# Cluster attention and a squared-ReLU MLP on one core: the three low bits of each weight are made on GpSimd, and VectorE joins them in one operation

## The chip, the cores and the metric

The kernel runs on one core of one Trainium2 chip. The metric is the device time in microseconds (us) of one execution; lower is better. Five engines of the core each work through their own queue of instructions in order: PE (TensorE, matrix products), DVE (VectorE), ACT (ScalarE), POOL (GpSimd) and SP (SyncE, which here issues the data transfers). They wait for one another by semaphores.

## The reference

Four batches of eight heads attend over 768 positions with a head size of 64; a query sees only the keys whose nearest of 16 centroids is its own. The result, 3072 rows of 512, goes through a two-layer MLP.

```python
q_assign = argmax(q_n . c_n);  k_assign = argmax(k_n . c_n)      # per head
scores = where(q_assign == k_assign, q @ k.T / sqrt(D), -1e9)
x = (softmax(scores) @ v).transpose(0, 2, 1, 3).reshape(B * S, H * D)
h = x @ w_in                       # w_in: 512 x 2048
g = s * relu(h) ** 2 + b
out = (g @ w_out).astype(float32)  # w_out: 2048 x 512
```

The weights `w_in` and `w_out` arrive as 64-bit floats (two 32-bit words each), all else in 32 bits. [...]

## The kernel before

**Weights.** The two matrices are cut into 16 pairs of tiles (`wi`, `wo`), 32 tiles of 128 x 512 values. `weights()` takes tile after tile through four steps: `fetch` loads both words of every value (512 KB) into a staging buffer; `rebase` (L213) lets ACT read the high words, 8 bytes apart, and put them as rebased floats into the tile; `narrow` (L217) lets DVE shift the tile left by three bits (L219) and then shift the low word right by 29 and OR it in (L220); `bound` (L223) takes absolute values on ACT (L227, L229) and column sums and maxima on PE and DVE (L232, L233). There are four staging buffers: three of the tag `stage`, and for every fourth tile the idle buffer `gs`. So a load has to wait until `narrow` of the tile four places ahead of it has read its buffer. When the last tile is through, scale factors for both matrices are known (`finish_w_in`, `finish_w_out`, into `glob`), and `wsplit` then splits each tile into two 16-bit parts (ACT L277, DVE L279), which the MLP's products use.

**Attention.** Work comes in 192 units (batch, chunk of 256 positions, pair of heads, tile of 128 rows, head). A unit's scores are made on PE (L476), their row maximum on DVE (L486), their exponential on ACT (L496). For the first 16 units the result is turned on PE into the one buffer `turned` (L520), half by half; each half is then copied by ACT (L525) and its remainder taken by DVE (L526). Later units are turned by DMA (L530) after a GpSimd subtraction (L528). `prep_k`, `prep_q` and `prep_v` load and split keys, queries and values and make the one-hot cluster codes (`onehot`, L298 to L304), which are written by GpSimd or DVE and turned by DMA into `KB` and `QB`.

**MLP.** Step m runs beside unit m + 21 (`LAG`): `mlp_in` (PE L632), `mlp_relu` (ACT L639 to L642), `mlp_gl` (POOL L647), `mlp_out` (PE L659). Its first step needs the first 16 units' output and the scale factors of the weights.

**Order.** The loop at the kernel's end names the work in program order. A scheduler then sets every engine's order by priorities and an estimated timeline of its own, so an edit at one place can move instructions of the whole first part of the program. SP's loads and DMA transposes stand in one queue in order.

Of the kernel before, what the change touches and what calls it, by code (L numbers as in the profile page):

```python
# [12 lines left out]
U32 = mybir.dt.uint32  # L13
AF = mybir.ActivationFunctionType
ALU = mybir.AluOpType
# [11 lines left out]
def tile_cluster_attention_mlp(ctx, tc, q, k, v, cent, w_in, w_out, s_in, b_in, out):  # L27
# [12 lines left out]
    V = nc.vector  # L40
    G = nc.gpsimd
# [171 lines left out]
    def rebase(d):  # L213
        hw = d["st"][:, :, :, 1].bitcast(F32)
        A.activation(d["w"], hw, AF.Prelu, scale=2.0 ** -112, alpha=-(2.0 ** 32))

    def narrow(d):  # L217
        c = d["w"].bitcast(I32)
        V.tensor_scalar(c, c, 3, None, op0=ALU.logical_shift_left)  # L219
        V.scalar_tensor_tensor(c.bitcast(U32), d["st"][:, :, :, 0].bitcast(U32), 29, c.bitcast(U32),  # L220
                               op0=ALU.logical_shift_right, op1=ALU.bitwise_or)

    def bound(d):  # L223
        w, p, ft = d["w"], d["p"], d["ft"]
# [14 lines left out]
    def weights():  # L239
        live = {}  # L240
        for i in range(2 * NF + 4):
            if 0 <= i - 4:
                bound(live[i - 4])
                narrowed[0] += 1
            if 0 <= i - 3 < 2 * NF:
                rebase(live[i - 3])
                narrow(live[i - 3])
            if i < 2 * NF:
                live[i] = fetch(i)
            if i < 2 * NF + 3:  # L250
                yield
# [571 lines left out]
```

## Time and profile before

| | |
|---|---|
| median of 3 runs | 946.23 us (946.06 to 949.96) |
| the profiled execution's own time | 952.97 us |
| its span, first to last instruction | 951.3 us |
| mean granted TensorE clock | 0.954 |
| busy share of the span: PE, DVE, ACT, POOL | 87%, 68%, 75%, 58% |

The profiled execution is one run of the program, 6.7 us above the median of the timed runs; 1.7 us of its time lie outside the span. A row of a timeline reads: start in us, duration in us, engine, line, operation, what is written from what, count, and in brackets the idle time of the engine just ahead with what ended it. A row of a group reads: engine and form, count, busy time and mean duration. In the table by stage each engine has its busy time and, in brackets, its number of instructions, followed by the granted clock of PE, the DMA engines' share and GB/s. "SPq" is SP's queue of transfers.

### The profile page before, as it was taken

To read this page: it belongs to the slowest core of one execution; us is meant where nothing else is said; L and a number is where in the kernel's file an instruction comes from. 1 tells how busy PE (TensorE), PEld (TensorE's weight loads), DVE (VectorE), ACT (ScalarE), POOL (GpSimd) and SP (SyncE) were. 2 spreads that over 40 slices of the span, in tenths; PEclk is the share of its full clock that TensorE was granted. 3 is DMA by queue.
4 is the path that set the end of the run, shared out by engine and by line. 5 is a ranking of instruction groups with operands and counts; after the bars stand their busy time and mean duration, and the time that the engine had idled before them with its cause. 6 is when DMAs were issued, how large, how long until landed. Compare 5 with 4: busy or idle time off the path is not lost.

```text
span 951.3 us, 22936 instructions
## 1 busy us (share of the span) xinstructions
PE 830.0 (87%) x8697; PEld 580.1 (61%) x8697; DVE 651.1 (68%) x1684; ACT 715.4 (75%) x1405; POOL 548.0 (58%) x580
## 2 busy tenths in 40 slices
PE   0565667886999889999999989999999899999997
PEld 0353445554676657767666657667766676676764
DVE  7689978798786766758967766667877565654100
ACT  3469866777688678788878868888888788888543
POOL 3010115667577567677677747767776676666321
PEclk9975697999999999999999999999999999999999
DMA  5898513767897897876887978979968777577200
GB/s 165 215 262 283 161 38 80 174 145 150 168 168 146 172 204 123 167 162 139 178 169 164 201 156 148 171 145 197 178 140 182 145 123 159 115 140 140 46 23 23
DMA packets 437759, 144.25 MB, mean 152 GB/s; under 512 B 405392, under 2 KB 434064, under 8 KB 437648
## 3 DMA queue, kind: packets, MB, share of 16 engines
q1 hardware_dynamic: 437648, 142.78, 70.7%
q8 instruction: 68, 1.11, 0.5%
q14 instruction: 43, 0.35, 0.1%
HBM read 35.69 MB, written 6.29 MB: 44 GB/s over the span
## 4 chain that ended last, share of the span: by engine, by line
PE 45%; DVE 23%; DMA 12%; ACT 7%; issue 5%; POOL 2%; SPq 1%; POOLq 0%; DVEq 0%; ACTq 0%
PE h L632 16%; PE acc L659 16%; PE sc L476 6%; DVE ssm L486 5%; DMA qn<-in_q_dram 3%; DMA PT<-ph 2%; PE sc L574 2%; DMA kn<-in_k_dram 2%; DMA vn<-in_v_dram 2%; PE sc L576 2%; PE sc L575 2%; ACT p L496 1%; DVE wis L279 1%; DVE qa L196 1%; DMA wst<-in_moe_w_in_dram 1%
## 5 line engine op out<-in xcount | busy, mean ns | idle before, releaser
L528 POOL TENSOR_TENSOR ph<-p,ph 128x768 f16<-128x768 f32 x176 | 297.0, 1688 | 129.7 <-ACT ph L126 71.1
L632 PE MATMUL h<-x,wis 128*128 128x256 f16 x2304 | 291.9, 276 | 16.1 <-ACT r L639 9.7
L659 PE MATMUL acc<-wos,gs 128*128 128x512 f16 x1152 | 299.7, 381 | 4.1 <-POOL gs L647 2.8
L632 PEld LDWEIGHTS <-wis 128*128 128x128 f16 x2304 | 222.5, 99 | 72.3 <-issue 18.0
L496 ACT ACTIVATE p<-sc,ssm,qsm 128x768 f32<-128x768 f32 x192 | 188.5, 982 | 2.0
L647 POOL TENSOR_TENSOR gs<-r,gs 128x256 f16<-128x256 f32 x192 | 136.5, 712 | 88.1 <-ACT r L642 79.4
L486 DVE TENSOR_REDUCE ssm<-sc 128x1 f32<-128x768 f32 x192 | 181.7, 947 | 2.8 <-PE sc L476 2.6
L659 PEld LDWEIGHTS <-gs 128*128 128x128 f16 x1152 | 101.4, 98 | 79.4 <-POOL gs L647 5.6
L493 ACT ACTIVATE ssm<-ssm,lift,qsm 128x1 f32<-128x1 f32 x192 | 73.1, 381 | 91.3 <-DVE ssm L486 90.1
L126 ACT ACTIVATE ph<-p 128x768 f16<-128x768 f32 x164 | 136.7, 833 | 1.3 <-DMA PT<-ph 0.2
L639 ACT ACTIVATE r<-h,cf 128x256 f32<-128x256 f32 x192 | 89.2, 465 | 57.8 <-PE h L632 54.5
L574 PE MATMUL sc<-vh,PT 128*128 128x65 f16 x1032 | 117.4, 195 | 6.9 <-DMA PT<-ph 6.8
L576 PE MATMUL sc<-vh,PT 128*128 128x65 f16 x1032 | 117.9, 193 | 0.0
L575 PE MATMUL sc<-vl,PT 128*128 128x64 f16 x1032 | 117.5, 192 | 0.0
L476 PE MATMUL sc<-KA,QA 128*128 128x384 f16 x384 | 98.9, 340 | 19.2 <-ACT p L496 13.8
L574 PEld LDWEIGHTS <-PT 128*128 128x128 f16 x1056 | 99.1, 98 | 22.8 <-DMA PT<-ph 10.1
L575 PEld LDWEIGHTS <-PT 128*128 128x128 f16 x1056 | 98.5, 99 | 11.8 <-issue 0.5
L476 PE MATMUL sc<-KB,QB 128*128 128x384 f16 x384 | 99.2, 340 | 6.9 <-DMA QB<-qb 6.9
L576 PEld LDWEIGHTS <-PT 128*128 128x128 f16 x1056 | 98.7, 97 | 1.3
L580 DVE TENSOR_SCALAR ssm<-sc 128x1 f32<-128x1 f32 x172 | 26.1, 152 | 84.5 <-PE sc L576 83.7
L642 ACT ACTIVATE r<-r 128x256 f32<-128x256 f32 x192 | 78.8, 410 | 2.9
L641 ACT ACTIVATE gs<-r 128x256 f16<-128x256 f32 x192 | 78.9, 411 | 2.7
(176 smaller groups left out, 1145.0 us busy)
## 6 DMA issues: line engine op xcount, KB each, us to landing
wst<-in_moe_w_in_dram SPq DMA_DIRECT2D x16, 512.0 KB, 5.1
kn<-in_k_dram SPq DMA_DIRECT2D x16, 384.0 KB, 4.3
qn<-in_q_dram SPq DMA_DIRECT2D x24, 256.0 KB, 3.3
vn<-in_v_dram SPq DMA_DIRECT2D x16, 384.0 KB, 4.3
out_dram<-o SPq DMA_DIRECT2D x12, 512.0 KB, 3.6
wst<-in_moe_w_out_dram SPq DMA_DIRECT2D x8, 512.0 KB, 5.7
gs<-in_moe_w_out_dram SPq DMA_DIRECT2D x8, 512.0 KB, 4.9
PT<-ph SPq DMA_TRANSPOSE x176, 3.4
```

Of the source, the lines that this page charges most:

```text
L126: A.activation(dst, src, AF.Copy)
L476: last_score[0] = nc.tensor.matmul(sc[:, e, :HALF], X[:, col, :], y[:, h * S + e * HALF : h * S + (e + 1) * HALF], start=st, stop=not st)
L486: last_max[0] = V.tensor_reduce(SM[i // 4][:, 0, j : j + 1], U[i]["sc"], axis=AX.XY, op=ALU.max, negate=True)
L496: last_exp[0] = A.activation(p.rearrange("p (a b) -> p a b", a=2), u["sc"], AF.Exp, bias=bi, scale=u["scale"], **total)
L528: G.tensor_tensor(u["ph"][:, 1, :], u["p"], u["ph"][:, 0, :], op=ALU.subtract)
L574: nc.tensor.matmul(o1, PT[:, kt, :], vh[:, h, kt, : D + 1], start=(kt == 0), stop=False)
L575: nc.tensor.matmul(o, PT[:, kt, :], vl[:, h, kt, :], start=False, stop=False)
L576: nc.tensor.matmul(o1, PT[:, T + kt, :], vh[:, h, kt, : D + 1], start=False, stop=(kt == T - 1))
L632: nc.tensor.matmul(ph[:, :CW], WSP[ft][0][:, wl, kt, :], XS[(b, c, kt)][:, :, xl, :], start=(i == 0), stop=(i == len(terms) - 1))
L639: A.activation(r, ph[:, :CW], AF.Relu, scale=MS[(b, c)][0])
L647: G.tensor_tensor(g[:, 1, :], r, g[:, 0, :], op=ALU.subtract)
L659: nc.tensor.matmul(acc[:, t, :], g[:, gl, rows], WSP[ft][1][:, wl, :], start=(ft == 0 and gl + wl == 0), stop=(ft == NF - 1 and gl == 1))
```

## The change

For each of the 32 weight tiles, `rebase` now also lets GpSimd turn the low words into the integers 0 to 7, in place in the staging buffer: a multiply and an add on the low word read as an unsigned integer, written as a 32-bit integer (rounded; the factor keeps the result in range). `narrow` is one DVE operation in place of two: it shifts the tile left by three bits and ORs these integers in.

```diff
@@ rebase, narrow @@
     def rebase(d):
         hw = d["st"][:, :, :, 1].bitcast(F32)
         A.activation(d["w"], hw, AF.Prelu, scale=2.0 ** -112, alpha=-(2.0 ** 32))
+        lw = d["st"][:, :, :, 0]
+        G.tensor_scalar(lw, lw.bitcast(U32), 0.9375 * 2.0 ** -29, -0.03125, op0=ALU.mult, op1=ALU.add)
 
     def narrow(d):
         c = d["w"].bitcast(I32)
-        V.tensor_scalar(c, c, 3, None, op0=ALU.logical_shift_left)
-        V.scalar_tensor_tensor(c.bitcast(U32), d["st"][:, :, :, 0].bitcast(U32), 29, c.bitcast(U32),
-                               op0=ALU.logical_shift_right, op1=ALU.bitwise_or)
+        V.scalar_tensor_tensor(c.bitcast(U32), c.bitcast(U32), 3, d["st"][:, :, :, 0].bitcast(U32),
+                               op0=ALU.logical_shift_left, op1=ALU.bitwise_or)
```

Lines below the added ones move by one (L486 becomes L487, and so on). The scheduler also orders the engines anew. Three places matter.

The first is DVE, where the first four weight tiles (`wi0`, `wo0`, `wi1`, `wo1`) come up, beside the one-hot codes of the first keys and queries (`om`, `oe`, `oo`). Before:

```order
L219 TENSOR_SCALAR wi0_257<-wi0_257 128x512
L302 TENSOR_REDUCE om_k0_0_296<-oe_k0_0_297 128x12
L219 TENSOR_SCALAR wo0_260<-wo0_260 128x512
L220 SCALAR_TENSOR_TENSOR wi0_257<-wst_0_258,wi0_257 128x512
L303 TENSOR_TENSOR oo_k0_0_298<-oe_k0_0_297,om_k0_0_296 128x192
L220 SCALAR_TENSOR_TENSOR wo0_260<-wst_1_261,wo0_260 128x512
L219 TENSOR_SCALAR wi1_263<-wi1_263 128x512
L304 TENSOR_SCALAR kb_132<-oo_k0_0_298 128x12x64
L220 SCALAR_TENSOR_TENSOR wi1_263<-wst_2_264,wi1_263 128x512
L219 TENSOR_SCALAR wo1_269<-wo1_269 128x512
L220 SCALAR_TENSOR_TENSOR wo1_269<-gs_128,wo1_269 128x512
L298 TENSOR_REDUCE om_q0_0_0_323<-pq_0_0_0_306 128x8
```

After, from the end of the second key's codes on:

```order
L305 TENSOR_SCALAR kb_1_140<-oo_k0_1_360 128x12x64
L487 TENSOR_REDUCE ssm_0_389<-sc_0_384 128x1
L221 SCALAR_TENSOR_TENSOR wo0_260<-wo0_260,wst_1_261 128x512
L487 TENSOR_REDUCE ssm_0_389<-sc_1_453 128x1
L221 SCALAR_TENSOR_TENSOR wi1_263<-wi1_263,wst_2_264 128x512
L221 SCALAR_TENSOR_TENSOR wo1_269<-wo1_269,gs_128 128x512
L128 COPY PT_0_462<-turned_135 128x384
```

Three of the four tiles' operations moved from among the first codes to behind the first row maxima (`ssm`).

The second place is DVE at the last weight tile (`wo15`). `sc_13` are the scores of unit 13, `PT_9` is the turned result of unit 9, in two halves. Before:

```order
L526 TENSOR_TENSOR PT_9_1020<-turned_135,PT_9_1020 128x384
L233 TENSOR_REDUCE w1_129<-pw_14_1332 128x1
L219 TENSOR_SCALAR wo15_1306<-wo15_1306 128x512
L486 TENSOR_REDUCE ssm_12_1153<-sc_13_1220 128x1
L220 SCALAR_TENSOR_TENSOR wo15_1306<-gs_128,wo15_1306 128x512
L233 TENSOR_REDUCE w1_129<-pw_15_1414 128x1
L526 TENSOR_TENSOR PT_9_1020<-turned_135,PT_9_1020 128x384
```

After:

```order
L527 TENSOR_TENSOR PT_8_927<-turned_135,PT_8_927 128x384
L221 SCALAR_TENSOR_TENSOR wi15_1298<-wi15_1298,wst_30_1299 128x512
L487 TENSOR_REDUCE ssm_12_1153<-sc_12_1148 128x1
L234 TENSOR_REDUCE w1_129<-pw_13_1289 128x1
L221 SCALAR_TENSOR_TENSOR wo15_1306<-wo15_1306,gs_128 128x512
L527 TENSOR_TENSOR PT_8_927<-turned_135,PT_8_927 128x384
```

The last weight tile now stands ahead of the second half of unit 8 and of unit 13's maximum, where it stood ahead of the second half of unit 9 and behind that maximum.

The third place is POOL in the middle of the weight stage. Before, the one-hot codes of keys 2 and 3 (`oe_k0_2`, `kb_2`, `oe_k0_3`, `kb_3`) stand there one behind the other:

```order
L301 TENSOR_TENSOR oe_k0_2_442<-oe_k0_2_442,rev_73 128x192
L304 TENSOR_SCALAR kb_2_143<-oo_k0_2_443 128x12x64
L301 TENSOR_TENSOR oe_k0_3_518<-oe_k0_3_518,rev_73 128x192
L304 TENSOR_SCALAR kb_3_146<-oo_k0_3_519 128x12x64
```

After:

```order
L302 TENSOR_TENSOR oe_k0_2_442<-oe_k0_2_442,rev_73 128x192
L217 TENSOR_SCALAR wst_6_483<-wst_6_483 128x512
L217 TENSOR_SCALAR gs_128<-gs_128 128x512
L305 TENSOR_SCALAR kb_2_143<-oo_k0_2_443 128x12x64
L217 TENSOR_SCALAR wst_8_559<-wst_8_559 128x512
L217 TENSOR_SCALAR wst_9_567<-wst_9_567 128x512
L217 TENSOR_SCALAR wst_10_629<-wst_10_629 128x512
L217 TENSOR_SCALAR gs_128<-gs_128 128x512
L302 TENSOR_TENSOR oe_k0_3_518<-oe_k0_3_518,rev_73 128x192
L217 TENSOR_SCALAR wst_12_671<-wst_12_671 128x512
L305 TENSOR_SCALAR kb_3_146<-oo_k0_3_519 128x12x64
```

The new operations stand between the code operations, which wait for DVE; each code operation that waits holds up the weight tiles behind it.

## The prediction

> **What bounds the kernel now.** I read first the table by stage, then the chain of waits of the weight stage, then SP's own waits, then single rows. The stages are the first codes (26 to 41 us), the weights (41 to 114), the way to the first MLP step (114 to 146), the splitting of the weights beside the MLP (146 to 240), and the rest.
>
> ```profile
> core 0: us, PE busy (x) PEld busy (x) DVE busy (x) ACT busy (x) POOL busy (x), PEclk, DMA share, GB/s
> 26.00:41.00 15.00, 5.29 (x55) 3.20 (x56) 11.32 (x29) 6.53 (x14) 0.00 (x0) 1.00 0.75 186
> 41.00:114.00 73.00, 45.46 (x361) 33.67 (x360) 64.50 (x149) 57.82 (x119) 7.07 (x9) 0.68 0.86 251
> 114.00:146.00 32.00, 20.83 (x234) 15.35 (x232) 25.25 (x70) 20.58 (x38) 5.56 (x6) 0.82 0.14 34
> 146.00:240.00 94.00, 75.48 (x764) 50.30 (x762) 81.94 (x183) 66.49 (x128) 61.30 (x53) 0.90 0.65 141
> 240.00:945.00 705.00, 679.26 (x7258) 475.74 (x7256) 447.35 (x1189) 553.88 (x1091) 463.97 (x470) 0.99 0.74 147
> ```
>
> From 240 us on PE is busy 96% of the time (679.26 of 705) and sets the end, whatever the change does. It can pay only by bringing that stage forward. Between 41 and 114 us, where all but four of the 32 tiles are narrowed, DVE is the fullest engine (64.50 of 73.00, 88%), but ACT has 79% and the DMA engines 86%, while POOL has 10%. The chain of waits of this stage says how these share the path:
>
> ```profile
> 42.08 4.57 DMA wst<-in_moe_w_in_dram
> ...
> 63.34 6.73 DMA wst<-in_moe_w_out_dram
> ...
> 92.33 5.29 DMA wst<-in_moe_w_out_dram
> ```
>
> Five times it runs through a load (the first, the longest and the last are shown), 25.5 us of the 73 in all; in the other 47 us it is on DVE, ACT and PE. The loads in turn wait for DVE to give back a staging buffer:
>
> ```profile
> SPq L86 <- DVE wi L220: 21.6, 10, 6.1
> SPq L86 <- DVE wo L220: 13.9, 7, 4.4
> ```
>
> So the weight stage is a ring: load, ACT, DVE, buffer free, load. A shorter DVE part shortens the ring, but the loads in it stay.
>
> **What is removed.** The 32 shifts (L219) go; the join (L220, now L221) stays with as many elements and inputs, so I give it the same price.
>
> ```profile
> L219 DVE TENSOR_SCALAR wi<-wi x16: 408/416/826, 27.0 to 109.1; 128x512 int32<-128x512 int32 x16
> L220 DVE SCALAR_TENSOR_TENSOR wi<-wst,wi x16: 671/679/843, 27.9 to 110.8; 128x512 uint32<-128x512 uint32 x16
> 63.19 0.41 DVE L219 TENSOR_SCALAR wi<-wi 128x512 int32<-128x512 int32 x1
> 63.53 0.34 DVE L303 TENSOR_TENSOR oo_k<-oe_k,om_k 128x192 f16<-128x192 f32 x1
> ```
>
> A shift is 0.41 us long, but the next instruction starts 0.34 us after it (63.19 to 63.53), so 0.34 is what each takes from DVE: 10.9 us for 32 (16 of `wi`, as many of `wo`).
>
> Four of them lie at 27 to 31 us. There the next thing DVE has to do waits for others:
>
> ```profile
> 37.76 1.82 DVE L486 TENSOR_REDUCE ssm<-sc 128x1 f32<-128x768 f32 x2 [1.76 <-PE sc L476]
> 41.43 0.56 DVE L128 COPY PT<-turned 128x384 f32<-128x384 f32 x1 [1.85 <-PE turned L520]
> ```
>
> DVE is idle for 1.76 and 1.85 us right behind, so these four are worth nothing, and the three joins that the change puts behind the first maxima fit into the 1.85. Without that cover the four shifts would be worth 1.4 us.
>
> Of the other 28 (9.5 us), nine start while the chain is on one of the five loads, from the first to the last of these:
>
> ```profile
> 59.93 0.41 DVE L219 TENSOR_SCALAR wi<-wi 128x512 int32<-128x512 int32 x1
> ...
> 95.88 0.42 DVE L219 TENSOR_SCALAR wi<-wi 128x512 int32<-128x512 int32 x1
> ```
>
> They only lengthen a queue that is not the last to end. Nineteen lie on the chain's other pieces: 19 x 0.34 = **6.5 us gained**. The bounds are 0 (the loads alone set the pace) and 10.9 (all 32 count).
>
> **What is added.** 32 operations on GpSimd, 128x512, one input, 32-bit integers 8 bytes apart. The trace has no such operation; the nearest rows are the last three of these, and the first is ACT's for the same tile:
>
> ```profile
> L215 ACT ACTIVATE wi<-wst 128x512 f32<-128x512 f32 x16 | 10.6, 666 | 7.4 <-DMA wst<-in_moe_w_in_dram 7.3
> L304 POOL TENSOR_SCALAR qb<-oo_q 128x512 f16<-128x512 f16 x23 | 14.2, 618 | 16.2 <-DVE oo_q L303 9.1 <-DVE ssm L580 2.9 <-DVE vm L443 2.1
> L128 POOL CAST ph<-p 128x768 f16<-128x768 f32 x3 | 2.5, 823 | 10.5 <-ACT p L496 10.5
> L528 POOL TENSOR_TENSOR ph<-p,ph 128x768 f16<-128x768 f32 x176 | 297.0, 1688 | 129.7 <-ACT ph L126 71.1 <-issue 18.1 <-PE acc L659 16.8
> ```
>
> The multiply-add on as many 16-bit elements takes 618 ns, and a cast that reads 32 bits is no slower per element (823 for 768). With two inputs it is 1688 for 768, 1125 ns for 512. I take 0.65 us, near the one-input rows, with 0.62 and 1.13 as ends. ACT needs 0.67 us for the tile, at the same time, so at this price the join waits no longer than it waited for ACT. The cover is gone if GpSimd is late: its queue is nearly empty (7.07 us of 73), but the operations behind a code operation that waits for DVE wait too, and behind a late join stand maxima and remainders that ACT and PE wait for.
>
> GpSimd at work costs DVE something. Here both meet:
>
> ```profile
> 105.61 0.67 POOL L599 TENSOR_TENSOR xn<-xs,xn 128x256 f16<-128x256 f32 x1 [25.90 <-ACT xn L596]
> 106.23 1.08 POOL L394 COPY qa<-qb 128x512 f16<-128x512 f16 x1
> ...
> 105.63 1.20 DVE L220 SCALAR_TENSOR_TENSOR wo<-gs,wo 128x512 uint32<-128x512 uint32 x1
> 106.76 0.83 DVE L219 TENSOR_SCALAR wi<-wi 128x512 int32<-128x512 int32 x1
> ```
>
> The join, 0.68 alone, takes 1.20 when it starts with a GpSimd operation of 0.67; the next GpSimd copy takes 1.08, and the shift behind it 0.83 in place of 0.41. [...] With the new work POOL is busy 7.07 + 28 x 0.65 = 25.3 us of some 68, 37%. A join then meets it in 37% of cases and waits half an operation, 0.33: 0.12 us each, on the chain 19 x 0.12 = **2.3 us lost**; the removed shifts no longer collide, but they met GpSimd seldom.
>
> [...]
>
> **What is moved.** At the last weight tile DVE has done one maximum and two remainders fewer than before (unit 13's maximum, halves of units 8 and 9). The weights no longer wait for these; they now come afterwards, where the turning of one half after another sets the pace:
>
> ```profile
> 49.28 0.87 DVE ssm L486
> 114.17 0.47 DVE PT L526
> ...
> 113.30 0.67 DVE L220 SCALAR_TENSOR_TENSOR wo<-gs,wo 128x512 uint32<-128x512 uint32 x1
> ...
> 121.17 0.56 DVE L526 TENSOR_TENSOR PT<-turned,PT 128x384 f16<-128x384 f32 x1 [0.92 <-ACT PT L525]
> 122.89 0.56 DVE L526 TENSOR_TENSOR PT<-turned,PT 128x384 f16<-128x384 f32 x1 [1.16 <-ACT PT L525]
> ```
>
> On the chain they take 0.87 and 2 x 0.47 us, 1.8 in all, by which the last join (113.30) comes earlier. Behind it a half takes 1.72 us, with DVE idle for 0.92 and 1.16. Two more cost 3.5 us: net **1.7 us lost** (0 if DVE's gaps take them up, 3.5 if the weights don't end earlier by the 1.8).
>
> **The sum.** 6.5 - 2.3 - 1.7 = 2.5 us. Against the profiled execution that is 951.3 to 948.8 of span, 952.97 to 950.5 of its time. The timed runs stand 6.7 us below this execution; the same 2.5 us off their median of 946.23 give **943.7 us**. About 0.5% (4.7 us) is what a measurement can tell here from no change, so this counts as none. I leave what the scheduler's other reorderings between 146 and 240 us do at zero, with some 3 us either way: DVE's 82 of 94 us there are the same operations, in slightly other places.
>
> **Rivals.**
>
> *DVE is the only bound.* The 88%, and SP's 35.5 us of waiting for DVE, speak for it; the five loads on the chain speak against. Then all 28 shifts pass on, the collisions cost 2.3, and the halves are made up for in DVE's gaps: 9.5 - 2.3 = 7.2, **939.0 us**.
>
> *GpSimd is dear.* If its operation takes 1.13 us, the two-input price, POOL is busy 38.7 us of 73 (53%). Each of the 28 joins waits 0.53 x 0.57 = 0.30 us, 8.5 us on all, and at the five places where the chain goes from a load to ACT the tile is ready 0.46 us later than by ACT, 2.3. With the moved halves: 6.5 - 8.5 - 2.3 - 1.7 = -6.0, 6 us slower, **952.2 us**. It decides from about 0.85 us an operation on, where 19 x 0.19 + 5 x 0.18 + 1.7 eats the 6.5. For it speaks that no 32-bit integer row on POOL stands in the trace; against it the two one-input rows, which agree. [...]
>
> *Loads and ACT set the pace.* DMA at 86% and ACT at 79% leave little: if the stage keeps its 73 us, the moved halves alone count, with half their price **947.1 us**. The loads that waited 35.5 us for DVE speak against.
>
> That the change does not do what it says I leave out: the order shows 32 new operations on POOL and none of the shifts.
>
> **The numbers.** My forecast has 0.38 (its own range 941 to 946.5), DVE as only bound 0.32, GpSimd dear 0.18, loads and ACT 0.12. Faster by over 0.5% (below 941.5): nearly all of the second and a little of the first, 0.34. Slower by over 0.5% (above 951): most of the third, 0.18, with the little that the reorderings may add. The rest, 0.48, is within 0.5%. For the range I go from between 939.0 and the bound of 935.3 (all 10.9 us) to just short of the dear case: 936.5 to 951.5.
>
> **What would show it.** The first MLP step is marked by its first activation:
>
> ```profile
> L639 ACT ACTIVATE r<-h,cf x192: 450/464/477, 151.2 to 943.1; 128x256 f32<-128x256 f32 x192
> ```
>
> Right: GpSimd's new row near 0.65 us; the joins at a mean near 0.8; the weight stage ending some 6 us earlier (the last join near 107 us, not 113); the first step's relu, which starts at 151.2 now, only 2 to 3 us earlier; the later stages of the same length. Wrong: a GpSimd row above 0.85 us with DVE idle for it; relu 7 us earlier or more, which would make DVE the only bound; or a last join at 113 us with DVE idle behind loads. A change of more than 3 us between relu and the end would mean that the new order matters more than the moved work.

## The result: 1.5% slower, and the loss comes in the long stage behind the weights

| | before | after |
|---|---|---|
| median of 4 runs | 948.1 us (946.06 to 950.62) | 962.27 us (960.67 to 964.61) |
| the profiled execution's own time | 952.97 us | 964.61 us |
| its span | 951.3 us | 962.9 us |
| mean granted TensorE clock | 0.954 | 0.947 |

The ratio is 1.0154, with a 95% interval of 1.0124 to 1.0183: 14 us slower, where 2.5 us faster was forecast. The kernel before has one run more here (950.62 us) than in the table ahead of the prediction, so its median is higher than the 946.23 us given there.

The new operation itself came out as it was priced. These are the changed kernel's rows for the GpSimd operation (L217), for the last joins (L221) and for the MLP's activations (L640), with the duration in ns as min/median/max and the first and last start in us:

```profile
L217 POOL TENSOR_SCALAR wst<-wst x24: 642/666/1202, 22.2 to 99.8; 128x512 int32<-128x512 uint32 x24
L217 POOL TENSOR_SCALAR gs<-gs x8: 642/655/988, 28.5 to 101.1; 128x512 int32<-128x512 uint32 x8
L221 DVE SCALAR_TENSOR_TENSOR wo<-wo,gs x8: 678/685/1154, 38.7 to 103.8; 128x512 uint32<-128x512 uint32 x8
L640 ACT ACTIVATE r<-h,cf x192: 450/465/477, 150.3 to 954.7; 128x256 f32<-128x256 f32 x192
```

GpSimd takes 0.65 us. The last join starts at 103.8 us, 9.5 us earlier than the 113.3 of before. But the first MLP activation starts only 0.9 us earlier (150.3 against 151.2), and the last one 11.6 us later (954.7 against 943.1). DVE hardly waits for GpSimd's result. These are all its waits for L217 in the whole program (total, times, longest, us):

```profile
DVE wi L221 <- POOL gs L217: 1.2, 1, 1.2
DVE wi L221 <- POOL wst L217: 1.2, 2, 0.8
DVE wo L221 <- POOL wst L217: 0.2, 1, 0.2
```

So the loss does not come from late results, and the first MLP step is not late either; the loss comes behind it. The table by stage, for 340 to 930 us, a stretch in which no weight tile is narrowed any more, shows the kernel before and then the changed one (length, then busy time and instructions of PE, PEld, DVE, ACT, POOL, the clock, DMA share, GB/s):

```profile
340.00:930.00 590.00, 569.77 (x6136) 400.87 (x6134) 373.32 (x1001) 469.46 (x924) 391.87 (x395) 1.00 0.74 148
```

```profile
340.00:930.00 590.00, 556.59 (x6006) 390.21 (x6004) 358.23 (x998) 459.21 (x904) 383.27 (x387) 0.99 0.74 146
```

PE is idle for 20.2 us of the 590 before and for 33.4 after: 13.2 us more, and it gets through fewer products (6006 against 6136). The same work can be compared from the 37th MLP activation to the last, again before and after:

```profile
337.60:943.10 605.50, 584.80 (x6241) 411.29 (x6241) 375.65 (x1005) 478.04 (x945) 397.62 (x402) 1.00 0.72 145
```

```profile
332.30:954.70 622.40, 588.99 (x6262) 412.43 (x6259) 361.45 (x1006) 477.50 (x945) 396.66 (x403) 0.99 0.72 141
```

That part takes 16.9 us longer in these two executions: PE is idle for 12.7 us more and busy for 4.2 us more, at a clock of 0.99 against 1.00. PE's waits from 240 to 945 us say what it stands still for, before:

```profile
PE h L632 <- ACT r L639: 7.4, 9, 2.5
PE sc L574 <- DMA PT<-ph: 6.8, 7, 1.7
PE sc L476 <- ACT p L496: 3.4, 3, 1.5
PE sc L476 <- DMA QB<-qb: 3.1, 3, 1.7
...
PE pq L407 <- DMA QA<-qa: 0.7, 1, 0.7
```

and after:

```profile
PE sc L477 <- ACT p L497: 7.6, 11, 1.6
PE sc L575 <- DMA PT<-ph: 6.5, 5, 2.7
PE pq L408 <- DMA QA<-qa: 5.9, 5, 2.2
PE acc L660 <- POOL gs L648: 3.3, 4, 1.1
PE h L633 <- ACT r L640: 3.2, 6, 0.9
PE pk L358 <- DMA KA<-ka: 2.7, 3, 1.4
...
PE acc L660 <- ACT gs L642: 2.2, 1, 2.2
```

All such rows together are 25.0 us in 34 waits before and 38.6 us in 46 waits after. No single wait became long (the longest is 2.5 us before and 2.7 after): there are more of them, and new kinds. PE now waits for the transposed queries ahead of `pq`, their products with the centroids (0.7 became 5.9), for the transposed keys ahead of `pk`, the same for keys, and for `gs` ahead of `acc`, the MLP's second product.

One of these stalls, followed back in the changed kernel's timeline (DVE, then SP's queue, then PE):

```profile
611.87 2.45 DVE L196 SCALAR_TENSOR_TENSOR qa<-qn,qsm,qb 128x256 f16<-128x256 f32 x2
...
614.39 1.23 SPq L399 DMA_TRANSPOSE QA<-qa  x1
...
618.60 0.18 PE L408 MATMUL pq<-cT,QA 128*128 128x16 f16 x1 [2.24 <-DMA QA<-qa]
...
618.71 1.11 PE L660 MATMUL acc<-wos,gs 128*128 128x512 f16 x3
```

The same block of queries before:

```profile
604.91 1.53 DVE L196 SCALAR_TENSOR_TENSOR qa<-qn,qsm,qb 128x256 f16<-128x256 f32 x2
...
606.50 1.23 SPq L398 DMA_TRANSPOSE QA<-qa  x1
...
614.14 0.17 PE L407 MATMUL pq<-cT,QA 128*128 128x16 f16 x1
```

Before, 7.6 us lie between the issue of the transpose and its first product, and PE does not wait. After, only 4.2 us lie between them, and 2.24 of these are a stall: the preparation came late relative to the place that `pq` has in PE's queue. None of the changed operations stands near; these instructions are the same in both kernels, and their order differs. In the changed kernel's last two rows PE runs nothing for 2.24 us, and the products of the MLP behind `pq` (`acc`, from 618.71 us) start only after it, without a wait of their own.

### The profile page after: what moved, and what is told of

Same layout as the page of the kernel before. It is cut to its first block, busy times and chain, and to the rows that moved or that the text cites. A ratio compares the mean times of both kernels' runs of the same rounds, so it can differ in the third digit from the quotient of the medians.

```text
span 962.9 us, 22962 instructions
## 1 busy us (share of the span) xinstructions
PE 834.0 (87%) x8697; PEld 579.9 (60%) x8697; DVE 626.7 (65%) x1652; ACT 715.0 (74%) x1405; POOL 569.6 (59%) x612
## 5 line engine op out<-in xcount | busy, mean ns | idle before, releaser
L660 PE MATMUL acc<-wos,gs 128*128 128x512 f16 x1152 | 305.4, 386 | 8.1 <-POOL gs L648 5.5
L487 DVE TENSOR_REDUCE ssm<-sc 128x1 f32<-128x768 f32 x192 | 181.8, 947 | 5.4 <-PE sc L477 4.6
L640 ACT ACTIVATE r<-h,cf 128x256 f32<-128x256 f32 x192 | 89.3, 465 | 76.0 <-PE h L633 67.6
L575 PE MATMUL sc<-vh,PT 128*128 128x65 f16 x1032 | 117.7, 196 | 6.5 <-DMA PT<-ph 6.5
L577 PE MATMUL sc<-vh,PT 128*128 128x65 f16 x1032 | 120.2, 194 | 0.0
L477 PE MATMUL sc<-KA,QA 128*128 128x384 f16 x384 | 99.3, 340 | 19.3 <-ACT p L497 13.2
```

The source lines that it names most:

```text
L477: last_score[0] = nc.tensor.matmul(sc[:, e, :HALF], X[:, col, :], y[:, h * S + e * HALF : h * S + (e + 1) * HALF], start=st, stop=not st)
L487: last_max[0] = V.tensor_reduce(SM[i // 4][:, 0, j : j + 1], U[i]["sc"], axis=AX.XY, op=ALU.max, negate=True)
L575: nc.tensor.matmul(o1, PT[:, kt, :], vh[:, h, kt, : D + 1], start=(kt == 0), stop=False)
L577: nc.tensor.matmul(o1, PT[:, T + kt, :], vh[:, h, kt, : D + 1], start=False, stop=(kt == T - 1))
L640: A.activation(r, ph[:, :CW], AF.Relu, scale=MS[(b, c)][0])
L660: nc.tensor.matmul(acc[:, t, :], g[:, gl, rows], WSP[ft][1][:, wl, :], start=(ft == 0 and gl + wl == 0), stop=(ft == NF - 1 and gl == 1))
```

## Experiments: order against arithmetic

Theory O: the scheduler's new order of the whole program costs the time, and the moved work does not. Theory M: the moved work costs it, through DVE operations that take longer beside GpSimd's (1.20 us for a join in place of 0.68, in the rows of the prediction) or through late results. To tell them apart, each engine's order of one kernel was recorded and forced on another by edges between neighbours that fix the order of issue and add no wait (the core of the code; the table of orders is left out):

```diff
+    for eng, perm in zip(engines, recorded()):
+        mine = [i for i in traced if i.engine == eng.engine and i.name not in FREE and type(i).__name__.startswith("Inst")]
+        for a, b in zip(perm, perm[1:]):
+            tc.add_manual_dep(mine[b], mine[a].name, nosync, reason="order")
```

`recorded()` unpacks the other kernel's order, and `FREE` holds the operation that the other kernel does not have. Every ratio below is to runs of the kernel before that were timed beside the run in question; their median was between 946.3 and 948.8 us.

**The changed arithmetic in the old order.**

```diff
+    FREE.add(g.ins.name)          # the GpSimd operation
+    pin(tc)                       # all others: the order of before
```

> The changed arithmetic, but every instruction of every engine stands in the order that the kernel before had (the GpSimd operation is the only one left free). Theory O, the new order of the whole program costs the time: the front keeps its gain (last join some 5 to 9 us earlier) and nothing is lost later, so 938 to 946 us against 948.1, ratio 0.990 to 0.998. [...]

947.25 us, ratio 1.0011 (0.9995 to 1.0028). The loss is gone, where theory M had it stay (958 to 966 us), so theory M falls. The gain is gone too, where theory O had expected 938 to 946 us. In the old order the last join still starts at 113.8 us. DVE's work from 41 to 114 us shrank from 64.50 to 58.75 us:

```profile
41.00:114.00 73.00, 47.34 (x355) 34.89 (x355) 58.75 (x120) 57.13 (x118) 29.00 (x37) 0.66 0.91 251
```

but its waits in that stretch grew by as much (9.5 us before, 15.3 now), among them

```profile
DVE om_q L306 <- POOL oe_q L305: 4.4, 1, 4.4
DVE PT L530 <- ACT PT L529: 3.0, 5, 1.1
...
DVE wi L224 <- POOL wst L219: 2.0, 2, 1.1
```

The first is a one-hot code on GpSimd that now stands behind a new operation there, which itself waits for its load:

```profile
68.98 0.66 POOL L219 TENSOR_SCALAR wst<-wst 128x512 int32<-128x512 uint32 x1 [3.92 <-DMA wst<-in_moe_w_in_dram]
69.72 0.46 POOL L305 TENSOR_TENSOR oe_q<-oe_q,rev 128x128 f32<-128x128 f32 x1
```

**The old arithmetic in the new order.**

```diff
+    FREE.add(s.ins.name)          # the VectorE shift
+    pin(tc)                       # all others: the order of the changed kernel
```

> The arithmetic of before (two VectorE operations, nothing new on GpSimd), with every other instruction in the order of the changed kernel. Theory O: it is as slow as the changed kernel or slower, since it has the order and not the shorter front: 960 to 972 us, ratio 1.013 to 1.025. Theory M: it is as fast as before, 945 to 951 us, ratio 0.997 to 1.003.

958.52 us, ratio 1.0119 (1.0089 to 1.0148). Theory O holds: without the change, its order alone costs 11 us. The time is just under the 960 to 972 us expected, and against expectation the changed arithmetic is not faster than the old one in this order (1.0154 against 1.0119). PE's busy time from 340 to 930 us is close to the changed kernel's:

```profile
340.00:930.00 590.00, 559.61 (x6063) 393.50 (x6060) 361.65 (x999) 461.77 (x911) 386.69 (x390) 1.00 0.73 147
```

**The two halves of the change, each alone in the old order.**

```diff
 # gpsimd_added_old_order: both VectorE operations stay
+        lw = d["st"][:, :, :, 0]
+        g = G.tensor_scalar(lw, lw.bitcast(U32), 0.9375 * 2.0 ** -29, -0.03125, op0=ALU.mult, op1=ALU.add)
 # no_shift_old_order: nothing on GpSimd
-        V.tensor_scalar(c, c, 3, None, op0=ALU.logical_shift_left)
```

> In the order of before, both VectorE operations stay and the GpSimd operation is added in place ahead of the join (the join then shifts a word whose bits are already at the bottom, so the three low bits of the weights are lost; nothing else changes). It prices the added operation alone. Theory O and the working of the prediction: 28 times 0.12 us of collisions at most, 1 to 4 us slower, ratio 1.001 to 1.004. Theory M: 10 us or more, ratio over 1.010.

> In the order of before, the VectorE shift is taken out and nothing is put in its place (the weights then have a wrong scale and the output is not the reference's). It prices the removed operation alone, the most that the change could bring. The prediction's working: 19 of 28 shifts on the path at 0.34 us, 4 to 8 us faster, ratio 0.992 to 0.996. If PE sets the end whatever the front does, or loads set the pace of the front: 0 to 2 us, ratio 0.998 to 1.000.

With the operation added: 951.9 us, ratio 1.0058 (1.0037 to 1.0079), 5.5 us slower and more than the 1 to 4 expected; the last join comes at 117.9 us. VectorE's operations there are the same as before and in the same order, and they take longer. The shifts before and then with the operation added (group rows for 0 to 150 us; behind the bar the busy time in us and the mean in ns):

```profile
L219 DVE TENSOR_SCALAR wi<-wi 128x512 int32<-128x512 int32 x16 | 7.1, 442 | 3.8 <-ACT wi L215 3.8
L219 DVE TENSOR_SCALAR wo<-wo 128x512 int32<-128x512 int32 x16 | 6.7, 416 | 3.1 <-ACT wo L215 3.1
```

```profile
L224 DVE TENSOR_SCALAR wi<-wi 128x512 int32<-128x512 int32 x16 | 9.1, 567 | 4.1 <-ACT wi L217 4.1
L224 DVE TENSOR_SCALAR wo<-wo 128x512 int32<-128x512 int32 x16 | 8.0, 501 | 1.2 <-ACT wo L217 1.2
```

So the 32 shifts go from 13.8 to 17.1 us, and the 32 joins from 23.1 to 25.7 us by the same rows: 5.9 us in all. VectorE's waits for GpSimd hardly count (0.3 us from 41 to 114 us). The changed kernel has no shifts, so the larger part of this price (3.3 us) does not arise in it.

With the shift removed: 945.63 us, ratio 0.9989 (0.9970 to 1.0008), 1 us faster and not clear of noise, where 4 to 8 were expected; the last join comes at 110.0 us. So in this order the shift was worth little. DVE's time there falls by 6.2 us,

```profile
41.00:114.00 73.00, 49.19 (x409) 37.71 (x409) 58.33 (x135) 60.08 (x125) 8.06 (x11) 0.67 0.88 252
```

and the weights end 3.3 us earlier. DVE waits for PE's scores instead (4.1 us, 0.8 before) and for ACT's half of `PT` (3.6 us, not among its waits before).

**Which part of the order?** Instructions of program step 57 and later (the 37th `relu` and later, from about 330 us) were given one kernel's order, the earlier ones the other's; the arithmetic is the changed one in both.

```diff
+    pin(tc)      # two chains an engine: steps below 57, steps from 57 on
```

> The changed arithmetic. Instructions that the program's text issues before its step 57 (weights, first tiles of the MLP, up to about 330 us) stand among themselves in the changed kernel's order, those of step 57 and later in the order of before. Theory T, the loss sits in the later order: PE's gaps after 240 us fall back from 38.7 to about 25 us, the first relu stays at 148 to 152 us, and the time is 940 to 948 us, ratio 0.993 to 1.002. Rival H, the new order of the front is what costs later (its clock or its buffers): 956 to 964 us, ratio 1.010 to 1.018.

> The counterpart: changed arithmetic, instructions before step 57 in the order of before (GpSimd's new operation free), those of step 57 and later in the order of the changed kernel. Theory T: 956 to 964 us, ratio 1.010 to 1.018, with 36 to 40 us of gaps on PE after 240 us. Rival H: 945 to 950 us, ratio 0.999 to 1.004.

The new front with the old tail: 941.36 us, ratio 0.9935 (0.9910 to 0.9960), **faster than both kernels**; PE's waits from 240 to 945 us are 26.7 us, near the 25 expected. The old front with the new tail: 959.49 us, ratio 1.0143 (1.0110 to 1.0176), with 33.4 us of such waits, a little under the 36 to 40 expected. The tail's order holds the whole loss. Behind the new front, the new tail against the old one is 1.0154 against 0.9935; behind the old front it is 1.0143 against 1.0011. That is 12 to 21 us for an order of the same instructions. PE's busy time from 340 to 930 us goes with the tail: 572.37 us with the old tail (569.77 in the kernel before), 562.03 with the new one (556.59 in the changed kernel).

Is that gain the change's, or the new front's? The same mixed order with the old arithmetic:

```diff
+    FREE.add(s.ins.name)          # the VectorE shift
+    pin(tc)                       # steps below 57: new order; from 57 on: old order
```

> The arithmetic of before, in the same mixed order that was fastest with the changed arithmetic (new order before step 57, old order from there on). Theory A, the gain of 6 us there is the change's, and the new order of the front only lets it through: last join near 111 us and first relu near 157 us as in the run of before in the new order, 945 to 952 us, ratio 0.998 to 1.005. Rival, the new order of the front is the better one by itself: 939 to 943 us, ratio 0.991 to 0.996.

944.3 us, ratio 0.9966 (0.9945 to 0.9988), between the two expectations. The new front's order brings about half of the gain by itself. The other half, 0.9966 to 0.9935 or some 3 us, would be the change's; the two intervals overlap a little, so it is not certain. By three pairs of runs, each pair with one order, the change by itself is therefore worth about 1 us slower (old order, 1.0011 against 1), 3 us slower (new order, 1.0154 against 1.0119) and 3 us faster (mixed order, 0.9935 against 0.9966), none of it clear of noise.

**Does it take the change to draw a bad order?** One useless copy, whose result nobody reads, was put into the kernel before at one weight tile (the diff shows the copy; `idle` is a new tile of 128x64 values):

```diff
     def narrow(d):
         c = d["w"].bitcast(I32)
+        if d["p"] == 12:          # 24 and 2 in the two other runs
+            V.tensor_copy(idle, d["w"][:, 0, :64])
```

> The kernel before with one VectorE copy of 128x64 elements more, at the thirteenth weight tile, whose result nobody reads; the scheduler is free. Its work is under 0.2 us, but the scheduler answers with an order that is close to the changed kernel's. Theory S, the change did no more than draw another order, and any small edit can do so: 955 to 963 us, ratio 1.009 to 1.018. Rival, the order needs the change's own operations to become slow: 945 to 950 us, ratio 0.999 to 1.004.

> The same copy at the twenty-fifth weight tile: the scheduler answers with a third order, which differs from both. Theory S has no sign for it: the orders of this program spread over some 15 us, so anywhere from 940 to 962 us; inside 0.3% of before (943 to 950 us) would mean that most orders are as good as that of before, over 955 us that the order of before was a lucky one.

> The control for the two runs with a small copy: the same VectorE copy of 128x64 elements in the kernel before, at the third weight tile, where the scheduler keeps the order of before (but for four VectorE instructions beside the copy). If the order is what costs, and not the copy: 945 to 949 us, ratio 0.998 to 1.002. If the copy itself, its wait or its buffer costs: ratio 1.005 or more, as the two others had.

At tile 12: 958.67 us, ratio 1.0125 (1.0096 to 1.0154). A copy of 64 elements a partition costs as much as the order of the changed kernel, because the scheduler answers it with an order close to that one. At tile 24, with a third order: 952.73 us, ratio 1.0052 (1.0029 to 1.0074), between the two signs that were named for it. At tile 2, where the order stays: 947.95 us, ratio 1.0001 (0.9984 to 1.0017). At that tile the copy itself costs nothing that can be measured.

The reverse is also to be had. In the changed kernel, with the scheduler free, the same copy at tile 6 leads to a tail close to the old one:

```diff
+        if d["p"] == 6:
+            V.tensor_copy(idle, d["w"][:, 0, :64])
```

> The changed kernel with no table of orders, and one useless VectorE copy of 128x64 elements more at the seventh weight tile. The scheduler then gives the part from step 57 on an order close to that of before. Theory S: the copy undoes the loss, 939 to 946 us, ratio 0.991 to 0.999. Rival, the change's own operations cost it: 956 us or more, ratio over 1.009.

941.89 us, ratio 0.9946 (0.9923 to 0.9969): as fast as the forced mixed order, and 2% (20 us) faster than the changed kernel, for one instruction whose result nobody reads.

**One piece of an order, priced.** On GpSimd, from step 57 on, each of 16 copies of a block of queries was put behind the next subtraction of a probability tile (`ph`). The edit is in the table of orders; at one of the 16 places the order changes like this:

```diff
-POOL COPY qa<-qb
 POOL TENSOR_TENSOR xn<-xs,xn
 POOL TENSOR_TENSOR ph<-p,ph
+POOL COPY qa<-qb
```

> The fastest mixed order, with one thing altered: on GpSimd each of the 16 copies of a Q block from step 57 on stands behind the next subtraction of a probability tile instead of ahead of it, as the changed kernel has it at 609 us. Theory L, a short helper operation that stands behind a long one on GpSimd stalls TensorE, since the block's score matmuls stand in its queue: each copy is 2 to 5 us later, TensorE's waits on the Q transpose grow by 1 to 3 us at each of the 16, 955 to 985 us, ratio 1.010 to 1.040. Rival, the slack ahead of those matmuls hides it: 940 to 945 us, ratio 0.992 to 0.998.

956.12 us, ratio 1.0085 (1.0058 to 1.0112), against 0.9935 without the edit: 14 us for 16 moves of one short instruction, about 0.9 us each. The direction is theory L's; the time is at the lower end of its range and the ratio just under it. PE's wait ahead of `pq` from 240 to 945 us, first without and then with the edit:

```profile
PE pq L410 <- DMA QA<-qa: 0.6, 1, 0.6
```

```profile
PE pq L410 <- DMA QA<-qa: 9.5, 8, 2.2
```

PE waits there eight times, not sixteen, and for 8.9 us more. The part from the 37th MLP activation to the last, first without and then with the edit:

```profile
328.50:933.10 604.60, 585.13 (x6261) 411.91 (x6258) 373.26 (x1005) 478.08 (x944) 397.59 (x402) 1.00 0.72 145
```

```profile
332.30:952.10 619.80, 589.74 (x6261) 412.66 (x6258) 376.61 (x1005) 478.31 (x944) 395.92 (x403) 0.99 0.69 142
```

It is 15.2 us longer: PE is idle for 10.6 us more, and busy for 4.6 us more with the same products, at a clock of 0.99 against 1.00. That execution has the lowest clock of the five with this edit (0.946 on the mean, and 962.04 us); the other four, at 0.960 to 0.966, still take 953.57 to 958.88 us, so the clock does not make the loss.

The landmarks side by side (us; one profiled execution each; the last column is the ratio of the timed runs):

| arithmetic, order | last join | first relu | PE busy, 340 to 930 | ratio |
|---|---|---|---|---|
| old, old | 113.3 | 151.2 | 569.8 | 1 |
| changed, new | 103.8 | 150.3 | 556.6 | 1.0154 |
| changed, old | 113.8 | 151.6 | 569.1 | 1.0011 |
| old, new | 111.3 | 157.9 | 559.6 | 1.0119 |
| changed, new front and old tail | 106.4 | 151.0 | 572.4 | 0.9935 |
| old, new front and old tail | 111.1 | 154.5 | 571.9 | 0.9966 |
| changed, old front and new tail | 110.4 | 148.1 | 562.0 | 1.0143 |
| old, with a copy at tile 12 | 111.2 | 155.5 | 561.1 | 1.0125 |
| changed, with a copy at tile 6 | 108.8 | 152.0 | 573.9 | 0.9946 |

In these rows the last two columns go together: under 563 us of PE work in that stretch, the kernel is slower by over 1%; with 569 or more it is as fast as before or faster. Of the other runs, the copy at tile 2 (569.5 us, 1.0001) and the kernel without the shift (569.2, 0.9989) fit, and the one with the late copies of queries nearly does (560.3, 1.0085). The copy at tile 24 lies between (567.4, 1.0052), and the run with GpSimd's operation added has 571.5 there and lost its 5.5 us in the front. The last join and the first relu, on which the prediction's sum rested, do not order the rows.

The granted clock, which the result's table shows lower after (0.947 against 0.954), does not order the kernels either. On the mean over its runs it is 0.957 both for the fastest mixed order (941.36 us) and for the old front with the new tail (959.49 us), and 0.958 for the kernel before timed beside them.

## Why the prediction was wrong, point by point

**The price of the GpSimd operation: right.** 0.65 us was taken, and the shortest and the median duration are 0.642 and 0.655 to 0.666 us. The rival that GpSimd is dear falls; that it alone forecast a slower kernel is chance.

**The collisions: they exist, and the joins' mean was about right.** The joins' busy times in the changed kernel are

```profile
L221 DVE SCALAR_TENSOR_TENSOR wi<-wi,wst 128x512 uint32<-128x512 uint32 x16 | 12.1, 758 | 3.0 <-POOL gs L217 1.2 <-POOL wst L217 1.2 <-ACT wi L215 0.3
L221 DVE SCALAR_TENSOR_TENSOR wo<-wo,gs 128x512 uint32<-128x512 uint32 x8 | 6.5, 813 | 0.0
L221 DVE SCALAR_TENSOR_TENSOR wo<-wo,wst 128x512 uint32<-128x512 uint32 x8 | 6.0, 750 | 0.4 <-POOL wst L217 0.2
```

or 0.77 us on the mean, near the 0.8 forecast. But the joins of the kernel before had a mean of 0.72 us already (23.1 us for 32), not 0.68, so the change made them longer by 0.05 us each. That a join which meets GpSimd waits half an operation (0.33 us, and 0.57 for a dear GpSimd), on which the 2.3 us and the rivals' collisions rest, was the author's estimate; no run shows it, and what the runs show in its place is these 0.05 us on the mean over all joins. The 5.5 us of the run with the operation added are no measure of this term, since the larger part of what VectorE lost there was in the shifts.

**6.5 us from 19 shifts: not so in the old order, and in the new one only for the last join.** With the order held, taking the shift away brought 1 us: the ring of load, ACT and DVE, and the waits for PE and ACT in between, filled the gap. There the rival that loads and ACT set the pace was the better description, since the last join stayed near 113 us (113.8 against 113.3). That its number (947.1) is close to what the changed arithmetic took in the old order (947.25) is chance: it counts halves of units that do not move in that order. In the new order the same change moved the last join from 111.3 to 103.8 us, but the whole time did not become shorter. The rival that DVE is the only bound falls in both orders: it asked for 7.2 us less, and in neither did the time become shorter. The two rivals also charge the collisions unevenly: the one of a dear GpSimd takes them on 28 joins where the forecast takes them on 19 (on 19 it would have given 949.4, not 952.2), and the one of DVE takes 28 shifts but the collisions of 19 joins (on 28 it would have given 940.1, not 939.0). How much of an engine's work lies on the path is a property of the order, and a chain of waits read from one order does not carry over to another.

**1.7 us lost at the end of the weights: mis-sized.** The weights ended 9.5 us earlier and the first relu came 0.9 us earlier, so 8.6 us were given back there. That too is the order's: with the old arithmetic the way from the last join to the first relu is 37.9 us in the old order (113.3 to 151.2) and 46.6 in the new one (111.3 to 157.9).

**The step that failed.** Two sentences: "From 240 us on PE is busy 96% of the time (679.26 of 705) and sets the end, whatever the change does", and the scheduler's other reorderings "between 146 and 240 us" put at zero, with 3 us either way. PE does set the end. But the 4% in which it was idle were a property of the order, not a constant, and the new order did not stop at 240 us, nor at the first part of the program, as the description of the scheduler ahead of the prediction has it: it reached to the last unit. That term was worth 11 us with the old arithmetic (1.0119 against 1) and 14 us with the changed one (1.0154 against 1.0011), more than all others together. The prediction's own sign for it, more than 3 us of change between the first relu and the end, showed clearly: 791.9 us became 804.4.

## What to carry to other kernels

Where a scheduler orders the whole program from an estimated timeline, an edit of a few microseconds draws a new order, and its luck can outweigh the edit: here a copy of 64 elements a partition cost 1.25% at one tile of one kernel, 0.5% and nothing at two others, and won back 2% at a tile of the other kernel. Price such a change against the same order (force the old order on it, or the new order on the old arithmetic) before judging the arithmetic; a change that looks 1.5% slower may by itself be worth next to nothing, as here, and have drawn a bad order. In a prediction, give the redrawn order a term and a width of its own, of the size that neutral edits show (here 0 to 1.25%), whatever engine is "the bound" afterwards.

## What was not expected of the hardware

Stalls repeat with the order. In four kernels with the new order in the tail or one close to it (the changed one, the old arithmetic in the new order, the old front with the new tail, the copy at tile 12), PE waits ahead of the same `pq` product at 618.6, 617.5, 615.9 and 616.7 us, for 2.2, 2.3, 2.9 and 2.0 us; no kernel with the old tail waits for a `pq` between 596 and 625 us. What DVE loses beside GpSimd may show far behind the moved work too: the two remainders `qa` that took 1.53 us at 604.91 us before take 2.45 us at 611.87 us after, with the longer of GpSimd's two kinds of subtraction beside them:

```profile
612.31 1.73 POOL L529 TENSOR_TENSOR ph<-p,ph 128x768 f16<-128x768 f32 x1
```

Before, the GpSimd operations beside them were of 0.67 to 0.84 us (from 604.74 to 606.97 us). That this is why they took longer was not tested by itself.
